# A Fourier mixing, RWKV channel-mix and Mish MLP kernel: tokens of each 128-group stored as (column, neighbour), output pieces written as 32 runs

## The chip, the cores and the metric

The kernel runs on one core of one Trainium2 chip. The metric is the device time of one execution in microseconds (us), median of three runs.

## What is computed

Three layers on `x` of shape (4, 3072, 256) in float32; the constants of the first one are real Fourier matrices.

```python
# 1: Fourier mixing over the sequence
X = rfft(x, axis=1)                       # per batch row and channel
Yr = Xr @ w_r - Xi @ w_i + b_r ; Yi = Xr @ w_i + Xi @ w_r + b_i
y = irfft(softshrink(Yr, 0.01) + 1j * softshrink(Yi, 0.01))
# 2: RWKV channel mix, y_prev is y shifted by one token
xk = mu_k * y + (1 - mu_k) * y_prev ; xr = mu_r * y + (1 - mu_r) * y_prev
k = relu(xk @ w_k) ; v = (k * k) @ w_v ; r = sigmoid(xr @ w_r)
z = r * v                                 # (12288, 256)
# 3: MLP
h = z @ w_in ; g = h * tanh(softplus(h))  # Mish
out = g @ w_out                           # (12288, 256)
```

## The kernel before

All matrix products run on TensorE in float32r with the operands split into a high and a low part (three products stand for one). The work goes through three stages, and each engine's instructions stand in the order in which the code writes them (`manual_schedule`).

**Stage 1**, up to about 310 us, does the forward transform, the mixing matrices and the first half of the inverse transform through scratch in DRAM (`scr1`, `scr2`).

**Stage 2**, about 310 to 982 us, does the second half of the inverse transform and the RWKV layer, with channels on the partitions and tokens along the free axis. It has 32 tiles of `TA` = 384 tokens. A tile is (batch b, j of 8); its 384 tokens are ordered (m, n, w): 3 groups of 128, and in each 4 neighbours n times 32 columns w. In the sequence the token of (m, w, j, n) is ((m · 32 + w) · 8 + j) · 4 + n, so the four neighbours of one column are four consecutive tokens. Per tile there are four pieces `P = 4t + i2`: `emit_k` makes two of the eight 128-wide slices of `k` into `kp` (L766, two buffers), `k_ev` makes `kr`, `kh`, `kl` of it (ScalarE L779, L789, L790, VectorE L791), and `emit_v(P - 2)` adds the slices to the value tile `vp` (L804, one buffer, two banks). `emit_r` (L743, piece 1) makes the receptance `pp`; `r_ev` (L752, piece 2) applies the sigmoid into `r` in SBUF (two buffers). `v_ev(t - 1)` (L812, piece 2) multiplies `r` of the tile before with `vp` on VectorE, and the GpSimd queue stores the product to `x2d` in DRAM (L813). In the order of TensorE the first value product of tile t (L804 of `emit_v(4t)`) stands behind the `kp` products of piece 2, and as `vp` has one buffer it waits for `v_ev(t - 1)`. On VectorE `v_ev(t - 1)` stands behind the `kl` of piece 1. Decoding of later weights (`bg_weight`, L117 to L136, of which L117, L121, L127 and L134 read every second 32-bit word of `dec_raw`) is put between these, one or a few operations at a time.

**Stage 3**, from 982 us, is the MLP over 24 blocks of 512 tokens: `h` by a seven-product scheme (L992, L995, L935 to L953), Mish on ScalarE (L973, L974), then `o` (L1040, L1041): four pieces of 128 tokens by 256 channels per block, with tokens on the partitions. At a block's end `o_out` copies (ScalarE L1055), adds (VectorE L1056) and has SyncE write each 128 KB piece to `out` (L1057); where its rows go is `out_v` (L895), indexed by batch, j and m. The last four pieces are the end of the program.

L331 and L332 stand in stage 1: L331 copies a block of 128 by 256, and L332 sets to zero, in place, eight elements per partition that lie 64 apart.

Of the kernel before, what the change touches and what calls it, by code (L numbers as in the profile page):

```python
# [12 lines left out]
AF = mybir.ActivationFunctionType  # L13
ALU = mybir.AluOpType
# [3 lines left out]
B, S, D, FK, FF = 4, 3072, 256, 1024, 2048  # L18
# [5 lines left out]
TA = 384  # L24
# [5 lines left out]
def kernel(  # L30
# [27 lines left out]
    nc = tc.nc  # L58
# [6 lines left out]
    def x2_part(c, n):  # L65
        q, o = divmod(c, 1536)
        return x2d[q][:, :, o:o + n]
# [358 lines left out]
    pp_t = {}  # L426
# [309 lines left out]
    def emit_r(t):  # L736
# [10 lines left out]
                    i += 1  # L747
        pp_t[t, "r"] = p

    def r_ev(t):  # L750
        r = pap.tile([128, 2, TA], F32, tag="r", name="r", bufs=2)
        nc.scalar.activation(out=r, in_=pp_t.pop((t, "r"))[:, :, 0:TA], func=AF.Sigmoid)  # L752
        r_t[t] = r

    kk_t, v_t = {}, {}
# [53 lines left out]
    def v_ev(t):  # L809
        p = v_t.pop(t)  # L810
        r = r_t.pop(t)
        nc.vector.tensor_tensor(out=r, in0=r, in1=p[:, :, 0:TA], op=ALU.mult)  # L812
        nc.gpsimd.dma_start(out=x2_part(TA * t, TA), in_=r)  # L813

    def pp():
# [3 lines left out]
    for t in range(NA + 1):  # L819
# [5 lines left out]
        for i2 in range(4):  # L825
# [7 lines left out]
            if nxt:  # L833
                if i2 == 0:
                    if put:
                        put()
                        put = None
                    if t > 0:
                        is2_ev(t + 1, 0)
                        is2(t + 1, 1, pp())  # L840
                elif i2 == 1:
                    if new:
                        split_Dp((t + 2) // 8)
                    if t > 0:
                        is2_ev(t + 1, 1)
                    delta()
                    if t + 2 < NA:
                        split_D(t + 2)
                elif i2 == 2:
                    if t > 0:  # L850
                        v_ev(t - 1)
                    r_ev(t)
                    if new:
                        prefix((t + 2) // 8, pp()[:, 0:2, :])
                    if t + 2 < NA:
                        split_IF(t + 2)
                    then = shift(t + 1, "xk")
                else:
                    if new:
                        put = prefix_ev()  # L860
                    if t + 2 < NA:
                        is2(t + 2, 0, pp())
                    then = shift(t + 1, "xr")
            elif i2 == 2:
                v_ev(t - 1)
                if live:
                    r_ev(t)
# [24 lines left out]

    pb = ctx.enter_context(tc.tile_pool(name="pb", bufs=1, side="left", reuse_waits="tile"))
    psb = ctx.enter_context(tc.tile_pool(name="psb", bufs=1, space=PSUM, reuse_waits="tile"))
    out_v = out.rearrange("(b m w j n) d -> b j m n w d", b=B, m=3, w=32, j=8)  # L895

    x2_t, o_t = {}, {}

# [164 lines left out]
    for P in range(2, 8 * NBLK + LAG):  # L1063
        t, q = divmod(P, 8)
# [103 lines left out]
```

## Time and profile before

| | us |
|---|---|
| median of three runs | 2007.17 (2006.61 to 2009.44) |
| span of the profiled execution | 2006.0 |
| TensorE busy in it | 1974.4 (98%) |
| VectorE busy | 1534.1 (76%) |
| ScalarE busy | 1149.5 (57%) |
| GpSimd busy | 28.1 (1%) |

The span is that of the instructions of one profiled execution, from the first to the last; the time of a run has about 1.2 us around it (2007.17 against 2006.0). In the rows PE is TensorE's matmul, PEld its weight load (which overlaps the matmul before), DVE VectorE, ACT ScalarE, POOL GpSimd and SP SyncE; a q behind the name is the engine's sequencer or DMA queue. An idle time in brackets names what ended it. A group's mean is that of one instruction in ns.

### The profile page before, as it was taken

How to read it: one execution, taken by the hardware profiler on the slowest of the kernel's cores; microseconds unless marked ns; L12 is line 12 of the kernel's file. 1: busy time of each engine (PE TensorE's matmuls, PEld its weight loads, DVE VectorE, ACT ScalarE, POOL GpSimd, SP SyncE). 2: the span in 40 equal slices, each digit the busy share in tenths (PEclk: the TensorE clock that was granted, in tenths of full speed). 3: DMA queues.
4: the chain of work that ended last, by engine and by line, in shares of the span. 5: the costliest groups of instructions: out<-in, count | busy, mean ns of one | idle time of the engine just before them, and what ended most of it. 6: DMA issues, size and time to landing. Idle time of an engine off the chain costs nothing.

```text
span 2006.0 us, 33418 instructions
## 1 busy us (share of the span) xinstructions
PE 1974.4 (98%) x13284; PEld 1890.9 (94%) x13284; DVE 1534.1 (76%) x2487; ACT 1149.5 (57%) x1703; POOL 28.1 (1%) x45
## 2 busy tenths in 40 slices
PE   6999999999999999999999999999999999999998
PEld 5999999999999999999989999999999999999997
DVE  6899997777776776775587778777787777877775
ACT  6666656777777777776544444444444444544443
POOL 0000000000000000000000000000000000000000
PEclk8999999999999999999999999999999999999999
DMA  8676532112121211111101000001010010000000
GB/s 265 181 214 201 168 111 90 53 58 70 49 80 49 65 62 58 60 49 46 37 22 32 22 25 30 22 22 33 22 33 22 22 33 22 28 27 22 22 12 22
DMA packets 71501, 123.19 MB, mean 61 GB/s; under 512 B 6192, under 2 KB 48432, under 8 KB 71344
## 3 DMA queue, kind: packets, MB, share of 16 engines
q1 hardware_dynamic: 67200, 106.49, 18.0%
q0 software_dynamic: 4144, 14.55, 1.9%
q8 instruction: 105, 1.72, 0.4%
q14 instruction: 52, 0.43, 0.1%
HBM read 70.69 MB, written 50.33 MB: 60 GB/s over the span
## 4 chain that ended last, share of the span: by engine, by line
PE 91%; DVE 4%; DMA 2%; ACT 1%; issue 1%; SPq 0%; DVEq 0%; ACTq 0%
PE h L992 20%; PE o L1040 17%; PE kp L766 13%; PE vp L804 13%; PE o L1041 9%; PE mxp L352 5%; PE p L992 3%; PE pp L743 3%; PE pp L458 3%; PE s2p L306 2%; PE s1p L265 1%; PE i1p L376 1%; DMA XS<-in_x_dram 1%; DMA A<-scr 1%; DVE Xl L77 1%
## 5 line engine op out<-in xcount | busy, mean ns | idle before, releaser
L1040 PE MATMUL o<-WO,gh 128*128 128x512 f32 x1536 | 562.5, 395 | 0.0
L1041 PE MATMUL o<-WO,gl 128*128 128x256 f32 x1536 | 430.5, 280 | 0.0
L992 PE MATMUL h<-xS,WS 128*128 128x256 f32 x2208 | 351.6, 281 | 0.0
L1005 ACT COPY p1s<-p 128x256 f32<-128x256 f32 x184 | 68.9, 374 | 470.9 <-PE p L992 469.9
L1040 PEld LDWEIGHTS o<-WO,gh 128*128 128x128 f32 x1536 | 289.1, 188 | 43.3
L992 PEld LDWEIGHTS h<-xS,WS 128*128 128x128 f32 x2208 | 300.4, 189 | 16.1
L766 PE MATMUL kp<-xk,WK 128*128 128x384 f32 x1536 | 291.3, 338 | 0.3 <-DVE yT L474 0.3
L1041 PEld LDWEIGHTS o<-WO,gl 128*128 128x128 f32 x1536 | 289.8, 189 | 0.2
L804 PE MATMUL vp<-kh,WV 128*128 128x384 f32 x1024 | 281.7, 336 | 0.0
L766 PEld LDWEIGHTS kp<-xk,WK 128*128 128x128 f32 x1536 | 267.5, 189 | 0.8 <-ACT Cs L388 0.8
L995 DVE TENSOR_TENSOR C<-h,p1s 128x512 f32<-128x512 f32 x184 | 127.2, 691 | 161.7 <-PE h L992 161.7
L791 DVE TENSOR_TENSOR kl<-kr,kh 128x768 fp32r<-128x768 f32 x128 | 122.9, 960 | 163.6 <-ACT kr L790 163.3
L977 DVE TENSOR_TENSOR gl<-g,gh 128x1024 fp32r<-128x1024 f32 x184 | 223.7, 1216 | 2.1 <-ACT g L974 2.1
L973 ACT ACTIVATE gh<-C 128x1024 fp32r<-128x1024 f32 x184 | 195.7, 1063 | 11.0 <-DVE C L995 11.0
L974 ACT ACTIVATE g<-C 128x1024 f32<-128x1024 f32 x184 | 193.0, 1049 | 0.0
L992 PE MATMUL h<-xS,WI 128*128 128x256 f32 x1104 | 190.4, 280 | 0.0
L995 DVE TENSOR_TENSOR C<-h,wu 128x512 f32<-128x512 f32 x368 | 187.6, 552 | 0.1
L804 PEld LDWEIGHTS vp<-kh,WV 128*128 128x128 f32 x1024 | 186.7, 188 | 0.0
L804 PE MATMUL vp<-kl,WV 128*128 128x384 f32 x512 | 171.7, 335 | 0.0
L789 ACT ACTIVATE kh<-kr 128x768 fp32r<-128x768 f32 x128 | 108.4, 847 | 88.0 <-PE vp L804 87.9
L992 PEld LDWEIGHTS h<-xS,WI 128*128 128x128 f32 x1104 | 156.0, 189 | 0.2 <-DVE xS L953 0.2
L995 DVE TENSOR_TENSOR wu<-h,C 128x512 f32<-128x512 f32 x184 | 126.6, 688 | 35.0 <-PE h L992 31.1
(152 smaller groups left out, 3136.7 us busy)
## 6 DMA issues: line engine op xcount, KB each, us to landing
A<-scr SPq DMA_DIRECT2D x48, 256.0 KB
scr<-Cs SPq DMA_DIRECT2D x48, 256.0 KB
D<-scr SPq DMA_DIRECT2D x32, 384.0 KB
x2d<-r POOLq DMA_DIRECT2D x32, 384.0 KB, 3.5
x<-x2d SPq DMA_DIRECT2D x24, 512.0 KB
out_dram<-ob SPq DMA_DIRECT2D x96, 128.0 KB
scr<-st SPq DMA_DIRECT2D x27, 384.0 KB
xs<-in_x_dram SPq DMA_DIRECT2D x24, 384.0 KB
```

The source lines that it names most:

```text
L352: nc.tensor.matmul(out=p[:, e, :], lhsT=a, rhs=WX[:, dh, c, w, :], start=(i == 0), stop=(i == 11))
L766: nc.tensor.matmul(out=p[:, m, 0:TA], lhsT=WK[:, dh, w, f * 128:(f + 1) * 128], rhs=hl[:, v, dh, :], start=(i == 0), stop=(i == 5),)
L789: nc.scalar.activation(out=kh, in_=kr, func=AF.Square)
L791: nc.vector.tensor_tensor(out=kl, in0=kr, in1=kh, op=ALU.subtract)
L804: nc.tensor.matmul(out=p[:, o, 0:TA], lhsT=WV[:, f, w, o * 128:(o + 1) * 128], rhs=v[:, m, :], start=(f == 0 and i == 0), stop=(f == 7 and ...
L973: nc.scalar.activation(out=gh, in_=c, func=AF.Mish)
L974: nc.scalar.activation(out=g, in_=c, func=AF.Mish)
L977: nc.vector.tensor_tensor(out=gl, in0=g, in1=gh, op=ALU.subtract)
L992: nc.tensor.matmul(out=out, lhsT=a(l), rhs=xS[:, v, b, :], start=(n == 0), stop=(n == 2))
L995: nc.vector.tensor_tensor(out=out, in0=x0, in1=x1, op=ALU.add)
L1040: nc.tensor.matmul(out=o[m], lhsT=gh[:, m2, ms], rhs=WO[:, f], start=(f == 0), stop=False)
L1041: nc.tensor.matmul(out=o[m][:, 0, :], lhsT=gl[:, m2, ms], rhs=WO[:, f, 0, :], start=False, stop=(f == 15))
```

## The change

Inside each group of 128 the 384 columns of `r` are stored as (w, n) in place of (n, w): column first, neighbour second. The views `nw` and `wn` address a plain and a reordered half tile in the same order of elements (m, n, w), so that the sigmoid reads `pp` in order and writes `r` with a step of four elements, and the multiply reads `vp` in order and reads and writes `r` with a step of four. Such a view has three free dims, so both operations are written once for each of the two halves `o`. The store to `x2d` and all that reads it are unchanged, but the partition index of an output piece is now (w, n). The output view takes the four neighbours of a column, four rows of 256 floats that follow each other in `out`, as one run of 1024 floats.

```diff
+    def nw(v):
+        return v.rearrange("p (m n w) -> p m n w", m=3, n=4)
+
+    def wn(v):
+        return v.rearrange("p (m w n) -> p m n w", m=3, n=4)
+
     def r_ev(t):
         r = pap.tile([128, 2, TA], F32, tag="r", name="r", bufs=2)
-        nc.scalar.activation(out=r, in_=pp_t.pop((t, "r"))[:, :, 0:TA], func=AF.Sigmoid)
+        p = pp_t.pop((t, "r"))
+        for o in range(2):
+            nc.scalar.activation(out=wn(r[:, o]), in_=nw(p[:, o, 0:TA]), func=AF.Sigmoid)
         r_t[t] = r
...
     def v_ev(t):
         p = v_t.pop(t)
         r = r_t.pop(t)
-        nc.vector.tensor_tensor(out=r, in0=r, in1=p[:, :, 0:TA], op=ALU.mult)
+        for o in range(2):
+            nc.vector.tensor_tensor(out=wn(r[:, o]), in0=wn(r[:, o]), in1=nw(p[:, o, 0:TA]), op=ALU.mult)
         nc.gpsimd.dma_start(out=x2_part(TA * t, TA), in_=r)
...
-    out_v = out.rearrange("(b m w j n) d -> b j m n w d", b=B, m=3, w=32, j=8)
+    out_v = out.rearrange("(b m w j n) d -> b j m w (n d)", b=B, m=3, w=32, j=8)
```

Lines behind the edit move: L752 becomes L760, L766 L774, L779 L787, L791 L799, L804 L812, L812 L821 and L1057 L1066. VectorE, at piece 2 of a tile in the middle of stage 2 (`kl` of piece 1, the multiply of the tile before, the split of the next `ifh`, the token shift `xf`), before:

```order
L791 TENSOR_TENSOR kl<-kr,kh 128x768 [waits PE_49,Activation_49]
L812 TENSOR_TENSOR r<-r,vp 128x768 [waits DMASW5_49,PE_49]
L77 TENSOR_TENSOR ifh<-ift,ifh 96x4x96 [waits DMAHW0_49,Activation_49]
L494 SCALAR_TENSOR_TENSOR xf<-dl,small,yT 128x384 [waits DVE_49]
L494 SCALAR_TENSOR_TENSOR xf<-dl,small,yT 128x384
```

The same place in the change:

```order
L799 TENSOR_TENSOR kl<-kr,kh 128x768 [waits PE_49,Activation_49]
L821 TENSOR_TENSOR r<-r,vp 128x3x4x32 [waits DMASW5_49,PE_49]
L821 TENSOR_TENSOR r<-r,vp 128x3x4x32
L77 TENSOR_TENSOR ifh<-ift,ifh 96x4x96 [waits DMAHW0_49,Activation_49]
L494 SCALAR_TENSOR_TENSOR xf<-dl,small,yT 128x384 [waits DVE_49]
L494 SCALAR_TENSOR_TENSOR xf<-dl,small,yT 128x384
```

The one multiply has become two of 384 elements at the same place, the second without a wait of its own; nothing else has moved.

TensorE at the same pieces (receptance, `kp` of piece 2, first value products), before:

```order
L743 MATMUL pp<-xr,WR 128x384 [waits DVE_49,Activation_49]
L743 MATMUL pp<-xr,WR 128x384 x11
L766 MATMUL kp<-xk,WK 128x384 x12
L804 MATMUL vp<-kh,WV 128x384 [waits DVE_49]
L804 MATMUL vp<-kl,WV 128x384
```

and in the change:

```order
L743 MATMUL pp<-xr,WR 128x384 [waits DVE_49,Activation_49]
L743 MATMUL pp<-xr,WR 128x384 x11
L774 MATMUL kp<-xk,WK 128x384 x12
L812 MATMUL vp<-kh,WV 128x384 [waits DVE_49,PE_49]
L812 MATMUL vp<-kl,WV 128x384
```

The order is the same; the first value product, which waits for VectorE's multiply of the tile before, names a semaphore of TensorE besides.

SyncE at the end of the program (loads of `x2d` and the output pieces), before:

```order
L901 DMA x_20155<-x2d_72 128x2x512
L1057 DMA out_dram<-ob 4x32x256 x4
L901 DMA x_20626<-x2d_72 128x2x512
L1057 DMA out_dram<-ob 4x32x256 x16
L1163 UNCONDITIONAL_BRANCH
```

and in the change:

```order
L910 DMA x_20219<-x2d_72 128x2x512
L1066 DMA out_dram<-ob 32x4x256 x4
L910 DMA x_20690<-x2d_72 128x2x512
L1066 DMA out_dram<-ob 32x4x256 x16
L1172 UNCONDITIONAL_BRANCH
```

No transfer has moved; the output's pattern is 32 by 4 by 256 in place of 4 by 32 by 256.

## Rows read from the trace of the kernel before

**Rows 1.** the page's head and part 1: busy time, share of the span, instructions.
```profile
span 2006.0 us, 33418 instructions
...
PE 1974.4 (98%) x13284; PEld 1890.9 (94%) x13284; DVE 1534.1 (76%) x2487; ACT 1149.5 (57%) x1703; POOL 28.1 (1%) x45
```

**Rows 2.** busy time by engine (instructions), clock, DMA share, GB/s, 300 to 978 us.
```profile
300.00:978.00 678.00, 675.76 (x4065) 673.18 (x4066) 473.93 (x790) 487.41 (x707) 23.42 (x32) 1.00 0.19 59
```

**Rows 3.** order of time, one tile: start us, us, engine, line, operation, idle before.
```profile
883.20 0.96 DVE L791 TENSOR_TENSOR kl<-kr,kh 128x768 fp32r<-128x768 f32 x1 [0.80 <-ACT kr L790]
883.28 2.24 PE L766 MATMUL kp<-xk,WK 128*128 128x384 f32 x12
883.48 0.81 ACT L752 ACTIVATE r<-pp 128x768 f32<-128x768 f32 x1 [0.31 <-PE pp L743]
884.07 0.95 DVE L812 TENSOR_TENSOR r<-r,vp 128x768 f32<-128x768 f32 x1
884.19 0.50 ACT L76 CAST ifh<-ift 96x384 fp32r<-96x384 f32 x1
...
885.19 0.19 PEld L804 LDWEIGHTS vp<-kh,WV 128*128 128x128 f32 x1
...
885.56 0.82 ACT L779 ACTIVATE kr<-kp 128x768 f32<-128x768 f32 x1 [0.87 <-PE kp L766]
```

**Rows 4.** all instructions of line 812: ns min/median/max, first and last start.
```profile
L812 DVE TENSOR_TENSOR r<-r,vp x32: 946/947/956, 347.5 to 982.1; 128x768 f32<-128x768 f32 x32
```

**Rows 5.** order of time at 964 us, then line 804's semaphore instruction.
```profile
964.63 0.95 DVE L812 TENSOR_TENSOR r<-r,vp 128x768 f32<-128x768 f32 x1
...
L804 PEldq EVENT_SEMAPHORE  x1: 51/51/51, 965.6 to 965.6; - x1
```

**Rows 6.** VectorE's groups by form: shapes, count | busy us, mean ns | idle.
```profile
L977 DVE TENSOR_TENSOR gl<-g,gh 128x1024 fp32r<-128x1024 f32 x184 | 223.7, 1216 | 2.1 <-ACT g L974 2.1
L995 DVE TENSOR_TENSOR C<-h,p1s 128x512 f32<-128x512 f32 x184 | 127.2, 691 | 161.7 <-PE h L992 161.7
...
L77 DVE TENSOR_TENSOR ifh<-ift,ifh 96x384 fp32r<-96x384 f32 x32 | 17.6, 549 | 1.6 <-ACT ifh L76 1.6
L935 DVE TENSOR_TENSOR xT<-x 128x256 f32<-128x256 f32 x46 | 17.3, 418 | 0.1
...
L131 DVE TENSOR_TENSOR dec_v<-dec_v,dec_b 128x512 f32<-128x512 f32 x25 | 17.2, 690 | 0.6
L121 DVE SCALAR_TENSOR_TENSOR dec_v<-dec_raw,dec_v 128x512 int32<-128x512 int32 x25 | 17.2, 687 | 0.3
```

**Rows 7.** order of time: two operations of line 935 on end, merged.
```profile
987.27 0.76 DVE L935 TENSOR_TENSOR xT<-x 128x256 f32<-128x256 f32 x2
```

**Rows 8.** ScalarE's groups by form, columns as in rows 6.
```profile
L468 ACT COPY yT<-yT 128x96 f32<-128x96 f32 x58 | 12.5, 263 | 0.0
...
L331 ACT CAST Xb<-Xh 128x256 fp32r<-128x256 f32 x4 | 1.6, 407 | 0.0
...
L332 ACT ACTIVATE Xb<-Xb 128x8 fp32r<-128x8 f32 x4 | 0.9, 220 | 0.1
```

**Rows 9.** order of time at the end of the program.
```profile
1996.79 2.64 SPq L1057 DMA_DIRECT2D out_dram<-ob  x4
...
1997.71 0.28 PE L1041 MATMUL o<-WO,gl 128*128 128x256 f32 x1
...
1998.43 0.42 DVE L1056 TENSOR_TENSOR ob<-ob,o 128x256 f32<-128x256 f32 x1 [0.28 <-ACT ob L1055]
```

**Rows 10.** stretches at the end, columns as in rows 2.
```profile
1997.50:1998.00 0.50, 0.49 (x4) 0.17 (x2) 0.27 (x1) 0.20 (x1) 0.00 (x0) 1.00 0.03 8
...
1999.00:2004.25 5.25, 0.00 (x0) 0.00 (x0) 0.00 (x0) 0.00 (x0) 0.00 (x0) 0.78 0.26 88
2004.25:2004.50 0.25, 0.00 (x0) 0.00 (x0) 0.00 (x0) 0.00 (x0) 0.00 (x0) 0.50 0.03 8
```

**Rows 11.** a stretch in which a 512 KB load of `x` moves.
```profile
1059.00:1059.50 0.50, 0.50 (x6) 0.50 (x5) 0.27 (x1) 0.00 (x0) 0.00 (x0) 1.00 1.04 401
```

## The prediction

> **What bounds the kernel now.** I read the page's first part, then the busy times of one long stage, then the order of time of one tile, then the last ten microseconds. The first part gives TensorE 98% of the span [rows 1]; in the receptance-and-value stage, 300 to 978 us, it is busy for 675.8 of 678 us [rows 2]. So an edit there costs nothing as long as TensorE is not made to wait, and each wait it adds lengthens the run by its full size. One tile of the 32 shows where such a wait would arise [rows 3]. The value tile `vp` has one buffer, so the first weight load of the next tile's values may start only when VectorE has multiplied the last tile out of it (L812). VectorE reaches L812 late, at 884.07, because it stands behind `kl` (883.20). It lasts 0.947 us [rows 4], so it ends at 885.02; the weight load that needs it comes at 885.19, and TensorE has no gap there. One tile has a weight load behind an added semaphore instruction [rows 5]: L812 ended at 964.63 + 0.95 = 965.58, the instruction stood at 965.60 and took 0.05, so a load could have gone 0.07 us after the multiply. The room is thus 885.19 − 885.02 − 0.07 = 0.10 us per tile. The second bound place is the end: after the last matmul only the four last output pieces remain.
>
> **Part 1: the multiply on VectorE.** One L812 of 768 elements becomes two of 384, `r` read and written with a step of four elements, `vp` read in order. First the split, with no price on the step. A plain 384-element operation takes 549 ns [rows 6]; two of one line issued together overlap, 0.76 us for two of 418 ns [rows 6, 7], that is by 0.08. So the pair takes 2 × 0.549 − 0.08 = 1.02 us, 0.07 more than the 0.947 it replaces. That is inside the room of 0.10: cost nothing.
>
> Then the step. No row of the kernel before shows a step of four elements. The nearest below is the decoding of weights: L121 reads a source with a step of two and takes 687 ns, where L131 without any step takes 690 [rows 6], so a step of two is free. The nearest above is L332 on ScalarE, eight elements 64 apart, read and written in place: 220 ns [rows 8]. From 263 ns for 96 elements and 407 for 256 the slope there is 0.90 ns and eight plain elements would take 263 − 88 × 0.90 = 184 ns, so the step cost about 36 / 8 = 4.5 ns an element. That is a rough end (two kinds of operation are compared), but the sign is against the change. On VectorE the slope is (1216 − 691) / 512 = 1.025 ns an element [rows 6]. Between an extra of zero and one of 4.5 ns I take one extra beat, 1.025 ns: four is nearer to two than to 64, but unlike the step of two it is used on the read and on the write at once, as L332 does. The pair then takes 1.02 + 768 × 0.001025 = 1.81 us, 0.86 more than now, and TensorE waits 0.86 − 0.10 = 0.76 us. 32 tiles are multiplied [rows 4], and behind 31 of them another tile's values wait: 31 × 0.76 = 23.6 us. Both ends kept: with no extra beat 0; with half a beat 31 × (0.46 − 0.10) = 11.2; with one and a half 31 × (1.25 − 0.10) = 35.7; with the 4.5 ns of L332 31 × (0.07 + 3.46 − 0.10) = 106 us. The last I do not believe, since it rests on eight elements.
>
> The Trainium skill speaks against this change: "Vector Engine (DVE) Microarchitecture Reference", section 5.2 "Measured stream behaviour on trn2", says that a port keeps its full rate only while elements come in runs of two adjacent words, and lists 1.71 to 2.51 ns per column for streams that hop at every element. The decode rows disagree with its wording for a step of two, which is free here; no row shows a step of four. By its figures (an estimate) the pair would be 0.60 to 1.21 us longer, and the run 15.4 to 34.4 us longer from this part.
>
> What queues behind it: on VectorE the `ifh` split, the `xf` operations and the `xk` split, none of which TensorE needs before the next tile; VectorE is busy 474 of 678 us [rows 2], so 0.86 us more in a tile of (982.1 − 347.5) / 31 = 20.5 [rows 4] fits. The store of `r` on the GpSimd queue is issued as much later; its reader starts after this stage. TensorE's wait names one semaphore more, for which the 0.05 us above is already taken.
>
> **Part 2: the sigmoid on ScalarE.** One operation of 0.81 us becomes two with a stepped write, started at 883.48 [rows 3]. At ScalarE's slope of 0.90 one extra beat is 0.69 us, and the split at most the fixed part, 263 − 96 × 0.90 = 177 ns [rows 8]: 1.68 us, to 885.16. The `ifh` cast (0.50) then ends at 885.66, where `kr` starts at 885.56 now, once its matmuls are ready [rows 3]. So `kr` comes up to 0.1 us late, and 0.8 with twice the extra; the `kp` buffer that it frees is one of two and is not written again before the piece after next, so at least one piece (a quarter of a tile, 5 us) later. `r` itself is wanted one tile later. Cost 0.
>
> **Part 3: the output pieces.** Under way they are hidden by the matmuls. At the end they are not: the last matmul starts at 1997.71, the last add ends at 1998.43 + 0.42 = 1998.85, the four issues stand from 1996.79 to 1999.43, data begins to move near 1998 and flows until 2004.25 at 88 GB/s and a DMA share of 0.26, a quarter of the 16 DMA engines [rows 9, 10], and is over in the quarter of a microsecond behind that. The transfer's outer count is four (4x32x256 in the order of SyncE's instructions). The load of `x`, whose outer count is 128, keeps a share of 1.04 and 401 GB/s [rows 11]. With 32x4x256 I expect it on all 16. The last piece is issued at 1998.9, behind its add, and, with the 1.2 us from issue to data of the first piece, moves from 2000.1; 128 KB at 401 GB/s are 0.33 us, at a slow start up to 0.9. Data ends near 2000.65 instead of 2004.25: −3.6 us (−3.3 to −3.8). What follows the last data stays. If the pieces stay on four engines: 0.
>
> **The sum.** The profiled execution spans 2006.0 us; the median of the runs is 2007.17, so 1.2 lie around it. 2006.0 + 23.6 − 3.6 = 2026.0, and with the 1.2 around it 2027.2 us, +1.0%.
>
> **Rivals.**
> (a) The step is free, as the step of two is. Then L812's pair ends 0.07 later, inside the room, and the end's gain is all: 2007.2 − 3.6 = 2003.6, not slower. The room is used up at an extra of 0.03 / 0.768 = 0.04 ns an element, and the two parts balance at (3.6 / 31 + 0.03) / 0.768 = 0.19 ns: that is the point from which the sign turns. For it: the decode rows. Against it: L332. The Trainium skill can be read this way too: "SBUF — State Buffer", "Door 1", speaks of lines of 16 bytes that want two hits each, and calls four fp32 the step that is still free; a step of four leaves one hit per line. By the first reading slower, by the second 2003.6. Chance 0.12 for free, and 0.04 for an extra so small that parts 1 and 3 cancel.
> (b) The step costs a beat or so, but the pieces stay on four engines, since the tile's side of the transfer still holds 128 rows of 1 KB: 2027.2 + 3.6 = 2030.8. Against it: the outer count did change. Chance 0.08.
> (c) Read and write penalties add: over one and a half extra beats, above 2007.2 + 35.7 − 3.6 = 2039.3. For it: both `r` streams step. Chance 0.12.
> (d) A small penalty of a quarter to half a beat: 2007.2 − 3.6 + 31 × 0.17 to 31 × 0.36 = 2008.8 to 2014.8. Chance 0.10.
> The forecast, half to one and a half beats with the end's gain: 0.54.
>
> **How the numbers follow.** 0.2% is 4.0 us, about what a measurement of this kernel can tell from no change. Rival (a) lies at −3.6, astride that line: of its 0.16 I give 0.06 to faster by over 0.2% and 0.10 to within 0.2%. All else is slower: 0.84. The range leaves out (a) and the far part of (c), 0.16 and 0.04: from 2009 to 2046 (an extra of 1.8 beats). The forecast's own range is 2014.8 to 2039.3.
>
> **What would show it.** L821 (the new line of the multiply) as 64 operations: about 0.95 us each for one extra beat, 0.55 if free. In the tile's order of time, the `vp` weight load right behind the second of them, with the idle before it put down to `r`; TensorE's busy share of the stage down by about 3%. The sigmoid's two at 0.8 to 0.9 us each, with `kr` still waiting for `kp`. At the end a DMA share near 1 and some 3.6 us less between the last add and the end of the span. The prediction is wrong if L821 is short, if VectorE reaches it earlier than now, or if `vp`'s load doesn't wait.

## The result, and the profile after

| | before | after |
|---|---|---|
| median of the runs, us | 2006.89 (4 runs) | 2022.51 (4 runs) |
| ratio, 95% interval | | 1.008, 1.0066 to 1.0094 |
| span of the profiled execution, us | 2006.0 | 2020.3 |

The change makes the kernel 15.6 us slower by the medians and 14.3 us by the two profiled spans. The head of the page after, and its part 1:

```profile
span 2020.3 us, 33517 instructions
...
PE 1983.1 (98%) x13284; PEld 1890.5 (94%) x13284; DVE 1555.0 (77%) x2519; ACT 1170.0 (58%) x1735; POOL 28.1 (1%) x45
```

TensorE is busy 8.7 us longer than in [rows 1] with the same number of instructions, and the span is 14.3 us longer. The longer time lies in stage 2: the 4065 products of 300 to 978 us [rows 2] now fill 300 to 996 us (columns as in rows 2):

```profile
300.00:996.00 696.00, 683.24 (x4065) 671.62 (x4065) 494.35 (x821) 508.26 (x738) 23.37 (x32) 1.00 0.18 57
```

Of these 18 us more, 7.5 are booked as busy time of TensorE (683.24 against 675.76), so its busy share alone shows too little of the delay. Where the time comes from is seen in one tile, in order of time (start us, us, engine, line, operation, idle before):

```profile
898.70 0.96 DVE L799 TENSOR_TENSOR kl<-kr,kh 128x768 fp32r<-128x768 f32 x1 [0.80 <-ACT kr L798]
898.79 2.25 PE L774 MATMUL kp<-xk,WK 128*128 128x384 f32 x12
898.98 1.55 ACT L760 ACTIVATE r<-pp 128x384 f32<-128x384 f32 x2 [0.32 <-PE pp L743]
899.57 1.61 DVE L821 TENSOR_TENSOR r<-r,vp 128x384 f32<-128x384 f32 x2
900.34 0.52 ACT L76 CAST ifh<-ift 96x384 fp32r<-96x384 f32 x1
901.07 0.81 ACT L787 ACTIVATE kr<-kp 128x768 f32<-128x768 f32 x1 [0.21 <-PE kp L774]
...
901.30 0.19 PEld L812 LDWEIGHTS vp<-kh,WV 128*128 128x128 f32 x1 [0.59 <-PE kp L774]
901.33 0.41 PE L812 MATMUL vp<-kh,WV 128*128 128x384 f32 x1 [0.30 <-DVE r L821]
```

These lines answer to [rows 3]. `kl`, the `kp` products and the sigmoid start at the same distances from each other as before, and the multiply starts 0.78 us after `kp`, before 0.79. But the pair of multiplies now lasts 1.61 us in place of 0.947 and ends at 901.18, and the `vp` weight load, which stood 1.91 us behind the start of `kp` (883.28 to 885.19), stands 2.51 us behind it (898.79 to 901.30), with idle time before it and before its product. The product's idle time is put down to `r`. The load's own 0.59 us are put down to `kp`, which had started long before; what came last is the multiply. The first product follows its load by 0.03 us now; before it was 0.17 us (885.19 to 885.36), so of the load's 0.60 us a part is made up again:

```profile
885.36 0.33 PE L804 MATMUL vp<-kh,WV 128*128 128x384 f32 x1
```

All the multiplies, with who waited for them, and three waits over the run (us in total, times, longest):

```profile
L821 DVE TENSOR_TENSOR r<-r,vp x64: 829/845/855, 348.5 to 1001.0; 128x384 f32<-128x384 f32 x64
...
  PE vp L812: 9.5, 31
```

```profile
PEld vp L812 <- PE kp L774: 17.9, 30, 0.8
...
PE vp L812 <- DVE r L821: 9.5, 31, 0.6
...
PE pp L458 <- DVE yT L474: 2.1, 1, 2.1
```

The third of them before:

```profile
PE pp L458 <- DVE yT L474: 1.4, 1, 1.4
```

There are 31 waits at `vp`, one behind each tile but the last, and one for `yT` at the start of the stage, 0.7 us longer than before. How much they cost in all is best read from the first and the last `kp` product, before and then after (ns min/median/max, first to last start):

```profile
L766 PE MATMUL kp<-xk,WK x1536: 331/334/525, 316.5 to 972.7; 128*128 128x384 f32 x192
```

```profile
L774 PE MATMUL kp<-xk,WK x1536: 331/334/522, 316.9 to 990.9; 128*128 128x384 f32 x192
```

656.2 us lay between them before, 674.0 now: 17.8 us more. With 0.7 us of it for the wait at `yT`, 17.1 are left for the 31 waits at `vp`, 0.55 us a tile. The stage starts 0.4 us later, and stage 3 takes the same to 0.2 us. At the end (the last add in order of time, then short stretches with DMA share and GB/s in the last two columns):

```profile
2016.45 0.42 DVE L1065 TENSOR_TENSOR ob<-ob,o 128x256 f32<-128x256 f32 x1 [0.28 <-ACT ob L1064]
```

```profile
2016.00:2016.50 0.50, 0.00 (x1) 0.00 (x0) 0.22 (x2) 0.37 (x1) 0.00 (x0) 1.00 0.77 260
...
2018.25:2018.50 0.25, 0.00 (x0) 0.00 (x0) 0.00 (x0) 0.00 (x0) 0.00 (x0) 1.00 0.91 311
2018.50:2018.75 0.25, 0.00 (x0) 0.00 (x0) 0.00 (x0) 0.00 (x0) 0.00 (x0) 1.00 0.08 21
2018.75:2019.00 0.25, 0.00 (x0) 0.00 (x0) 0.00 (x0) 0.00 (x0) 0.00 (x0) 1.00 0.00 0
```

The last add ends at 2016.45 + 0.42 = 2016.87 and the span 3.43 us later; before, it was 1998.85 and 2006.0 [rows 1, 9], 7.15 us. Data now moves at up to 311 GB/s and a share of 0.91, and is over soon after 2018.5, 1.65 us behind the last add, where it went on for 5.4 us at 88 GB/s and 0.26 [rows 10]. So 17.8 − 3.7 + 0.4 − 0.2 = 14.3 us, the whole difference of the spans.

### The profile page after: what moved, and what is told of

Its sections match the earlier page's. It is cut to its first block, busy times and chain, and to the rows that moved or that the text cites. A ratio compares the mean times of both kernels' runs of the same rounds, so it can differ in the third digit from the quotient of the medians.

```text
span 2020.3 us, 33517 instructions
## 1 busy us (share of the span) xinstructions
PE 1983.1 (98%) x13284; PEld 1890.5 (94%) x13284; DVE 1555.0 (77%) x2519; ACT 1170.0 (58%) x1735; POOL 28.1 (1%) x45
## 3 DMA queue, kind: packets, MB, share of 16 engines
q1 hardware_dynamic: 68352, 106.49, 17.4%
q8 instruction: 105, 1.72, 0.4%
## 4 chain that ended last, share of the span: by engine, by line
PE 50%; DVE 1%; ACT 1%; issue 0%
PE h L1001 19%; PE o L1049 17%; PE o L1050 9%; PE p L1001 3%; PE vp L812 0%; PE h0p L709 0%; DVE gl L733 0%; DVE ws L929 0%; ACT gh L731 0%; ACT g L732 0%; DVE wa L923 0%; ACT WS L76 0%; PE hp L709 0%; PE kp L774 0%; DVE xS L956 0%
## 5 line engine op out<-in xcount | busy, mean ns | idle before, releaser
L812 PE MATMUL vp<-kh,WV 128*128 128x384 f32 x1024 | 283.9, 338 | 9.5 <-DVE r L821 9.5
L774 PE MATMUL kp<-xk,WK 128*128 128x384 f32 x1536 | 291.5, 338 | 0.3 <-DVE yT L474 0.3
L774 PEld LDWEIGHTS kp<-xk,WK 128*128 128x128 f32 x1536 | 267.5, 189 | 0.8 <-ACT Cs L388 0.7
L799 DVE TENSOR_TENSOR kl<-kr,kh 128x768 fp32r<-128x768 f32 x128 | 122.9, 960 | 160.8 <-ACT kr L798 159.3
L812 PEld LDWEIGHTS vp<-kh,WV 128*128 128x128 f32 x1024 | 186.8, 188 | 18.6 <-PE kp L774 17.9
L812 PE MATMUL vp<-kl,WV 128*128 128x384 f32 x512 | 171.8, 336 | 0.0
```

What stands on the lines that cost most here:

```text
L774: nc.tensor.matmul(out=p[:, m, 0:TA], lhsT=WK[:, dh, w, f * 128:(f + 1) * 128], rhs=hl[:, v, dh, :], start=(i == 0), stop=(i == 5),)
L799: nc.vector.tensor_tensor(out=kl, in0=kr, in1=kh, op=ALU.subtract)
L812: nc.tensor.matmul(out=p[:, o, 0:TA], lhsT=WV[:, f, w, o * 128:(o + 1) * 128], rhs=v[:, m, :], start=(f == 0 and i == 0), stop=(f == 7 and ...
```

## The experiments

The theory behind all of them: the price is the multiply's step of four elements, paid by TensorE because the multiply ends behind the moment at which the next tile's first `vp` weight load is due; the output view gives back 3.7 us at the end; all else hides. Rivals: the second instruction, the stepped sigmoid, or the output view cost or give something else. Ratios are against runs of the kernel before on the same chip.

**The output view alone.**

```diff
-    out_v = out.rearrange("(b m w j n) d -> b j m n w d", b=B, m=3, w=32, j=8)
+    out_v = out.rearrange("(b m w j n) d -> b j m w (n d)", b=B, m=3, w=32, j=8)
```

> The kernel before with the changed output view alone (32 rows of 1024 floats); tokens stay in (neighbour, column) order, so the rows of the output land in another order than the reference's. Theory (the multiply's step costs 17 us in 31 waits of TensorE, the output view gives 3.7 us back at the end): 3.7 us faster than the kernel before, ratio 0.9982, the end of the span 3.4 us behind the last add instead of 7.15. Rival (the end is bound by something else, and the 14 us of the profiles are the step's cost less nothing): within 1 us of the kernel before.

2002.82 against 2007.25 us, ratio 0.998 (0.9971 to 0.9988). The page's head and the last add in order of time:

```profile
span 2000.6 us, 33418 instructions
```

```profile
1996.81 0.42 DVE L1056 TENSOR_TENSOR ob<-ob,o 128x256 f32<-128x256 f32 x1 [0.28 <-ACT ob L1055]
```

From the end of the add, 1997.23, to the end of the span are 3.4 us, as after the change. The theory's 3.7 us lie inside the interval (2.4 to 5.8 us); the rival is out. The two profiled spans differ by more, 5.4 us. The other 1.6 us need not be the output view's, since the granted clock differs in stage 2: over 330 to 345 us it was 0.89 in the profile before, so TensorE was at 1.2 GHz for a part of it, and 1.00 here. By an estimate from these two figures that is 0.11 × 15, about 1.6 us. Before, then here:

```profile
330.00:345.00 15.00, 13.57 (x75) 13.28 (x75) 11.66 (x20) 10.04 (x16) 0.00 (x0) 0.89 0.18 48
```

```profile
330.00:345.00 15.00, 13.58 (x84) 13.29 (x83) 11.84 (x21) 11.60 (x18) 0.00 (x0) 1.00 0.16 44
```

The profiles of the kernel before and of the changed one can be compared in this stretch: both were at 0.89.

**The split alone, with the output view of before.**

```diff
+        for o in range(2):
+            nc.scalar.activation(out=r[:, o], in_=p[:, o, 0:TA], func=AF.Sigmoid)
...
+        for o in range(2):
+            nc.vector.tensor_tensor(out=r[:, o], in0=r[:, o], in1=p[:, o, 0:TA], op=ALU.mult)
```

> The kernel before with the sigmoid and the multiply written as two halves each, without a step, and its own output view. Theory: the pair of multiplies lasts 1.02 us, inside the room of 0.10 us, so within 1 us of the kernel before. Rival (the second instruction and the added semaphore of TensorE cost, not the step): 31 waits of 0.2 to 0.5 us, 6 to 17 us slower.

2007.52 against 2007.25, ratio 0.9999 (0.999 to 1.0008). The instructions of the multiply and the sigmoid, then TensorE's semaphore instructions at the `vp` loads:

```profile
L821 DVE TENSOR_TENSOR r<-r,vp x64: 545/548/555, 345.3 to 980.5; 128x384 f32<-128x384 f32 x64
```

```profile
L760 ACT ACTIVATE r<-pp x64: 485/490/495, 325.5 to 962.4; 128x384 f32<-128x384 f32 x64
```

```profile
L812 PEldq EVENT_SEMAPHORE  x1: 51/51/51, 963.7 to 963.7; - x1
```

The multiplies take 548 ns each, as the prediction took from the `ifh` split of the same size, and no time lost: two instructions fit into the room. The other half of the rival, the added semaphore, is not tested here: one load has a semaphore instruction, as in the kernel before [rows 5], where the change has 31. The run with the step on the other side, below, tests it.

**The multiply one piece earlier,** with the step kept.

```diff
                     delta()
                     if t + 2 < NA:
                         split_D(t + 2)
+                    if t > 0:
+                        v_ev(t - 1)
                 elif i2 == 2:
-                    if t > 0:
-                        v_ev(t - 1)
                     r_ev(t)
```

> The changed kernel with the multiply of the tile before recorded one piece earlier, ahead of kl of piece 1 on VectorE; same operations, same step. Theory (only the end of the multiply against the vp weight load matters): the pair still lasts 1.61 us but ends over a microsecond before the load; no wait is left, and with the end's 3.7 us the time is 3 to 4 us under the kernel before, about 2003. Rival 1 (the stepped sigmoid on ScalarE or the longer VectorE work as such costs): stays 10 us or more above the kernel before. Rival 2 (the multiply now delays kl, and kl delays something that TensorE wants): a new wait, 5 us or more above 2003.

2005.64 against 2007.25, ratio 0.9992 (0.9983 to 1.0001). One tile in order of time:

```profile
759.19 1.62 DVE L821 TENSOR_TENSOR r<-r,vp 128x384 f32<-128x384 f32 x2
...
760.73 0.95 DVE L799 TENSOR_TENSOR kl<-kr,kh 128x768 fp32r<-128x768 f32 x1
...
762.66 0.19 PEld L812 LDWEIGHTS vp<-kh,WV 128*128 128x128 f32 x1
```

The pair still takes 1.62 us, but it now runs ahead of `kl` and ends 1.85 us before the `vp` load, which has no idle time. The same operations and the same step, with nothing changed but the place, are some 17 us faster than the changed kernel: the step costs only where its end is waited for. The forecast for this run, 3 to 4 us under the kernel before, was a little too good; measured are 1.6, and the interval ends just short of 3.7. Of the 2.1 us that are missing, 0.8 are visible in TensorE's waits in stage 2, in this kernel and then in the split alone:

```profile
PE pp L458 <- DVE yT L474: 2.0, 1, 2.0
...
PE vp L812 <- DVE r L821: 0.3, 1, 0.3
```

```profile
PE pp L458 <- DVE yT L474: 1.5, 1, 1.5
```

The wait for `yT` in the first tiles is 0.5 us longer. One wait at `vp` of 0.3 us is left, at 967.8 us: it belongs to the last tile, where the multiply kept its old place. What the remaining microsecond is stays open; it is within what runs of one kernel differ by.

**The step on the other side:** `r` in order in SBUF, PSUM read with a step of 32.

```diff
+    def ps(v):
+        return v.rearrange("p (m n w) -> p m w n", m=3, n=4)
+    def mwn(v):
+        return v.rearrange("p (m w n) -> p m w n", m=3, n=4)
...
+            nc.scalar.activation(out=mwn(r[:, o]), in_=ps(p[:, o, 0:TA]), func=AF.Sigmoid)
...
+            nc.vector.tensor_tensor(out=mwn(r[:, o]), in0=mwn(r[:, o]), in1=ps(p[:, o, 0:TA]), op=ALU.mult)
```

> The changed kernel with the step on the other side: r is written and read in order in SBUF, and the sigmoid and the multiply read PSUM with a step of 32 elements. Theory 1 (the price belongs to SBUF accesses): pair 1.02 us, sigmoid 0.45 us each, time 3.7 us under the kernel before, 2003. Theory 2 (any access whose elements lie apart costs, in PSUM too): pair 1.6 us or more, time as the changed kernel or above, 2020 to 2030.

2004.01 against 2007.25, ratio 0.9982 (0.9973 to 0.9991): the same computation with the same output runs as the change, and faster than both kernels. One tile in order of time, then the instructions of the multiply and the sigmoid and TensorE's semaphore instructions at the `vp` loads:

```profile
883.85 0.96 DVE L802 TENSOR_TENSOR kl<-kr,kh 128x768 fp32r<-128x768 f32 x1 [0.80 <-ACT kr L801]
...
884.73 1.01 DVE L824 TENSOR_TENSOR r<-r,vp 128x384 f32<-128x384 f32 x2
...
885.86 0.19 PEld L815 LDWEIGHTS vp<-kh,WV 128*128 128x128 f32 x1
```

```profile
L824 DVE TENSOR_TENSOR r<-r,vp x64: 546/548/556, 347.8 to 983.2; 128x384 f32<-128x384 f32 x64
```

```profile
L763 ACT ACTIVATE r<-pp x64: 485/490/495, 326.5 to 965.1; 128x384 f32<-128x384 f32 x64
```

```profile
L815 PEldq EVENT_SEMAPHORE  x31: 51/51/51, 348.9 to 966.3; - x31
```

The pair takes 1.01 us, ends at 885.74, and the load at 885.86 has no idle time. Theory 1 holds: reading PSUM with a step costs nothing here, neither on VectorE (548 ns a half, as in the split alone) nor on ScalarE (490 ns a half, as in the split alone too, where 450 had been expected and the stepped write took 884). The 31 semaphore instructions of the change are there and cost nothing either. The load comes 0.12 us behind the multiply, and in the changed kernel, where it waits, it comes 0.12 us behind it too (901.18 to 901.30): the plain pair just fits, with next to nothing to spare.

**A step of two,** by both views cut by two; one of them is shown.

```diff
-        return v.rearrange("p (m w n) -> p m n w", m=3, n=4)
+        return v.rearrange("p (m w n) -> p m n w", m=3, n=2)
```

> The changed kernel with the views cut by two in place of four, so that r is stepped by two elements (inner runs of 64); the output lands in another order of tokens than the reference's. Theory (the price comes with the distance, and a step of two is free as in the weight decoding): multiplies of 0.55 us each, sigmoids of 0.49, no wait of TensorE, 3.2 to 4.4 us under the kernel before, about 2003. Rival (any element that stands alone pays): 0.85 us each and the time of the changed kernel, 2022.

2004.34 against 2007.49, ratio 0.9984 (0.9974 to 0.9993). The multiply and the sigmoid:

```profile
L821 DVE TENSOR_TENSOR r<-r,vp x64: 548/549/556, 348.3 to 983.7; 128x384 f32<-128x384 f32 x64
```

```profile
L760 ACT ACTIVATE r<-pp x64: 505/521/525, 326.9 to 965.7; 128x384 f32<-128x384 f32 x64
```

549 ns on VectorE: a step of two is free there, for the read and the write together. ScalarE's stepped write takes 521 ns in place of 490; the expected 490 was a little too good.

**The step in the sigmoid alone.**

```diff
-            nc.vector.tensor_tensor(out=wn(r[:, o]), in0=wn(r[:, o]), in1=nw(p[:, o, 0:TA]), op=ALU.mult)
+            nc.vector.tensor_tensor(out=r[:, o], in0=r[:, o], in1=p[:, o, 0:TA], op=ALU.mult)
```

> The changed kernel with the step in the sigmoid alone: the multiply's two halves read and write r in order, so the product mixes the receptance of one token with the value of another. Theory (ScalarE's longer sigmoid hides): sigmoids 0.88 us each as in the changed kernel, multiplies 0.55, no wait at vp, 3 to 4 us under the kernel before, 2003. Rival (part of the 17 us comes through ScalarE): over 2008.

2004.69 against 2007.49, ratio 0.9986 (0.9977 to 0.9996).

```profile
L760 ACT ACTIVATE r<-pp x64: 861/886/923, 329.0 to 968.3; 128x384 f32<-128x384 f32 x64
```

```profile
L821 DVE TENSOR_TENSOR r<-r,vp x64: 547/548/556, 350.9 to 986.1; 128x384 f32<-128x384 f32 x64
```

```profile
PE pp L458 <- DVE yT L474: 2.1, 1, 2.1
```

For comparison the sigmoid of the changed kernel:

```profile
L760 ACT ACTIVATE r<-pp x64: 859/884/906, 326.6 to 982.4; 128x384 f32<-128x384 f32 x64
```

The sigmoid is as long as in the changed kernel (886 ns against 884) and makes no tile wait. What it does cost is the longer wait for `yT` at the start of the stage, 2.1 us as in the changed kernel: 0.7 of the 17.8 us, and no more.

**The read alone, and the write alone,** each in place of the multiply of the change.

```diff
+            nc.vector.tensor_tensor(out=nw(p[:, o, 0:TA]), in0=wn(r[:, o]), in1=nw(p[:, o, 0:TA]), op=ALU.mult)
```

```diff
+            nc.vector.tensor_copy(out=wn(r[:, o]), in_=nw(p[:, o, 0:TA]))
```

> The changed kernel with a multiply that only reads r with a step and writes its product in order back to PSUM; what is stored is the receptance alone. For the length of one multiply of 384 elements, not for the time. If read and write pay at once, side by side: 0.85 us as with both. If the write alone pays: 0.55. If the two add: between, near 0.70.

> The changed kernel with a copy of vp in order from PSUM into r with a step of four in place of the multiply; what is stored is the value without the receptance. For the length of one operation of 384 elements. If read and write pay side by side: 0.85 us. If the read alone pays: 0.55. If the two add: near 0.70.

One run each. The instructions of the read alone, then of the write alone:

```profile
L821 DVE TENSOR_TENSOR vp<-r,vp x64: 832/842/853, 349.5 to 1005.6; 128x384 f32<-128x384 f32 x64
```

```profile
L821 DVE COPY r<-vp x64: 829/841/884, 349.5 to 999.5; 128x384 f32<-128x384 f32 x64
```

842 and 841 ns against 845 with both. Read and write pay the same price side by side, and taking the step from one of them saves nothing. The write alone is a copy, and a plain copy of 384 elements was not run; from the 678 ns of the copies of 512 elements out of PSUM in the kernel before and 1.025 ns an element it would take about 547 (an estimate):

```profile
L276 DVE COPY st<-s1p 96x512 f32<-96x512 f32 x8 | 5.4, 678 | 0.0
```

The run of the write alone took 2020.32 us, near the changed kernel. That of the read alone took 2026.01, more, as its two halves of 842 ns do not overlap; the pair, then the `kp` products:

```profile
882.18 1.72 DVE L821 TENSOR_TENSOR vp<-r,vp 128x384 f32<-128x384 f32 x2
```

```profile
L774 PE MATMUL kp<-xk,WK x1536: 331/334/522, 317.9 to 995.3; 128*128 128x384 f32 x192
```

The first and the last of these lie 677.4 us apart, 21.2 more than before, or 20.6 without the longer wait for `yT` (2.0 us here, 1.4 before). A pair of 1.72 us gives 31 × (1.72 − 0.947 − 0.10) = 20.9: the sum of the prediction holds at another length of the pair too.

**A step of three and of sixteen.**

```diff
-        return v.rearrange("p (m w n) -> p m n w", m=3, n=4)
+        return v.rearrange("p (m w n) -> p m n w", m=1, n=3)
```

```diff
-        return v.rearrange("p (m w n) -> p m n w", m=3, n=4)
+        return v.rearrange("p (m w n) -> p m n w", m=3, n=16)
```

> The changed kernel with the views cut into three runs of 128 per half, so that r is stepped by three elements; the output lands in another order of tokens than the reference's. For the length of one multiply. If the price is all or nothing once an element has no neighbour in reach of a step of two: 0.85 us as with four. If it grows with the share of elements that start a new stretch of four words (three in four with a step of three, half with two, all with four): between 0.55 and 0.85, near 0.70. If three is still free: 0.55.

> The changed kernel with the views cut by sixteen, so that r is stepped by sixteen elements (inner runs of eight); the output lands in another order of tokens than the reference's. For the length of one multiply. If each element that stands alone pays one fixed price: 0.85 us as with four. If the price grows with the distance, as the 4.5 ns an element of the eight-element operation of the kernel before would have it: over 1.0 us, and the time over 2028.

Again both views are cut and one is shown. One run each; the multiply with three, then with sixteen, and the sigmoid in the same order:

```profile
L821 DVE TENSOR_TENSOR r<-r,vp x64: 652/672/684, 349.7 to 991.4; 128x384 f32<-128x384 f32 x64
```

```profile
L821 DVE TENSOR_TENSOR r<-r,vp x64: 806/823/833, 347.6 to 998.5; 128x384 f32<-128x384 f32 x64
```

```profile
L760 ACT ACTIVATE r<-pp x64: 666/690/702, 328.1 to 973.1; 128x384 f32<-128x384 f32 x64
```

```profile
L760 ACT ACTIVATE r<-pp x64: 844/866/902, 327.3 to 979.9; 128x384 f32<-128x384 f32 x64
```

The runs took 2012.53 and 2019.19 us, against 2006.37 for one run of the kernel before.

Over the 548 ns of the plain half the step of two adds nothing, three adds 124 ns, four 297 and sixteen 275: per element 0, 0.32, 0.77 and 0.72 ns. The price is reached at four and does not grow with the distance. A step of three pays a part of it, as it would if the element's neighbour in the same stretch of four words decided: of four elements then two stand alone in their stretch, with a step of two none and with four all. Half of 297 would be 149 ns; 124 were measured, so this way of counting is near and not exact. (The expectation counted the elements that start a new stretch, three in four between half and all, which gives the same 149 ns.) The Trainium skill has that stretch: "SBUF — State Buffer", "Door 1", speaks of 16-byte lines that want two hits for the full rate. These four runs agree with its sentence on two hits, and not with its reading that a step of four fp32 words is still free.

## Why the prediction was right, and by how much it was off

The forecast was 2027.2 us, 20.0 above the median it started from; measured were 2022.51, 15.6 above the median of the four runs before. Step by step:

- **Where the path is.** TensorE is bound in stage 2, the only end that matters is that of the multiply, and the room is 0.10 us. Held: with the measured pair of 1.61 us the room leaves 1.61 − 0.947 − 0.10 = 0.56 us a tile, 31 × 0.56 = 17.4; measured 17.1 of the 17.8 between the first and the last `kp` product. That the room fits so well is in part luck. The 0.07 us from the multiply to a waiting load were 0.12, which leaves the load a room of 0.05 and moves it by 0.60 us (1.91 to 2.51); the first product, closer behind its load than before, makes up about 0.05 of that (0.55 us a tile are left), and this was not foreseen.
- **The split.** Taken at 0.07 us within the room. Held: the pair of plain halves is 1.01 us long in the kernel that reads PSUM with a step, and the split alone costs nothing, though the pair uses up the room.
- **The step.** This term was mis-sized. One extra beat, 1.025 ns an element, was taken between the free step of two and the 4.5 ns worked out from L332; measured are 0.77 ns, three quarters of a beat, so 0.56 instead of 0.76 us a tile and 17.1 instead of 23.6 us. The upper end from L332 was far off: from four to sixteen the price doesn't grow with distance, nor does it on ScalarE (884 ns with four, 866 with sixteen, about 1.0 ns an element over the plain 490). What the 36 ns there belong to is open; a step of 64 was not run. The figures that the Trainium skill lists for VectorE streams that hop at every element ("Vector Engine (DVE) Microarchitecture Reference", section 5.2), 1.71 to 2.51 ns per column, hold 1.025 + 0.77 = 1.80 ns near their lower end; the part by them, 15.4 to 34.4 us, holds the 17.1.
- **The sum of read and write.** Rival (c) had the two add up. Out: each alone costs as much as both.
- **The sigmoid.** Expected at 0.8 to 0.9 us a half and hidden, cost 0. Held at 0.884 in the tiles; at the start of stage 2 it costs 0.7 us in the wait for `yT`, a place that the prediction did not look at.
- **The end.** −3.6 expected, −3.7 in the profiles, −4.4 by the medians of the run with the output view alone. With a DMA share of up to 0.91 the pieces do not stay on a quarter of the engines; rival (b) is out.
- **What would show it.** The multiply at 0.95 us each was expected for one beat and 0.55 if free; 0.845 lies where three quarters of a beat put it. The wait stands right behind the second half, as described. Only the books differ: the load's idle time is put down to `kp` and the product's to `r`. TensorE's busy share of the stage was to fall by about 3%; it fell from 675.76 of 678 to 683.24 of 696 us, by 1.5 points, since a part of the delay is booked as busy.

Rival (a), a free step, would have given 2003.6; the runs in which the step is free or hidden came out at 2004.0 to 2005.6, up to 2.0 above it.

## What to carry to other kernels

Read the cost of a longer operation from the distance between its end and the start of what waits for it: here 0.10 us of room or less in a tile of 20.5 decided between nothing and 0.9% of the run. When elements must be reordered, put the step on the side on which it is free (here the PSUM read), or do the work where nobody waits for it. An output transfer's outer count is worth a look wherever it ends the program: four against 32 was 3.7 us.

## What the runs showed of the hardware

Reading PSUM with a step of 32 elements costs nothing on VectorE (548 ns a half, as plain) and on ScalarE (490 ns, as plain). In SBUF a step of two float32 elements is free on VectorE (549 ns for 384 elements, 548 in order); three takes 672, four 845 and sixteen 823, and with four it does not matter whether one operand or both are stepped (842, 841 and 845 ns). ScalarE's stepped write goes much the same way, but pays a little with two: 490 in order, 521, 690, 884 and 866 ns. The last output pieces moved at a DMA share of 0.26 with an outer count of four, and of up to 0.91 with 32.
